# Two buffers for the folds' key and query weights in place of four, two more for the perceptron's weight sums, and earlier loads for both

## The chip, the cores and the metric

The kernel runs on one core of a Trainium2 chip. The metric is the device time of one execution in microseconds (us); the median of three runs of the kernel before is 1908.61 us (1908.29 to 1909.63). TensorE does the matmuls, VectorE (DVE), ScalarE (ACT) and GpSimd (POOL) work on tiles in SBUF, and SyncE (SP) issues nearly all DMAs. Each engine takes its instructions strictly in the order in which the program lists them, so an instruction that waits holds up everything behind it on the same engine; for SP that means that a DMA that may not start yet holds up every DMA listed after it.

## The reference

A pre-norm block on 2048 tokens of width 1024: linear attention with 32 heads, whose queries and keys go through a small matrix per head and two softmaxes (of p and of -p), then a perceptron of width 3584 with ReLU. Inputs and outputs are float32.

```python
qkv = x_normed @ wqkv                                  # heads of 32
pq, pk = q @ w_phi[h], k @ w_phi[h]
phi = concat(softmax(p), softmax(-p))                  # for pq and pk
kv, z = phi_k^T v, sum over tokens of phi_k
o = (phi_q kv) / (phi_q z + 1e-6)
h = x + o @ wo
out = h + relu(layernorm(h) @ w1) @ w2
```

## The kernel before, in words

TensorE multiplies in a 32-bit format with shortened mantissas (`F32R`), so each operand is split into a high and a low part and each product takes three matmuls (`mm3`, lines 181 to 184): high by high, high by low, low by high. The second one (line 183) is the first to read the low part of the weights.

**Steps and items.** All work is listed by hand in the order of "items". An item of the first phases is one output tile of 128 tokens by 512 columns and has 8 "steps"; a step is one `mm3`, that is three matmuls of 512 columns. `when(step, f, ...)` lists the call `f` behind the matmuls of the step with that number. Items 0 to 31 (steps 0 to 255) compute keys and values of the first eight token tiles, eight items for each of four column groups s; items 32 to 47 (steps 256 to 383) the queries, in two column groups; then keys and values, and queries, of the other eight tiles; then attention, output projection and the perceptron. So the weights change at steps 64, 128, 192, 256 and 320.

**Weights.** `Units` loads a 128x512 piece of weights into one of 6 `raw` buffers (lines 324 and 325 for keys and values, 328 for queries), ACT copies its high part into one of 10 `w` buffers (line 125), and POOL or DVE, in turn, subtracts to get the low part (line 129). Eight `w` are in use by the eight items of a column group, so two of the next group's pieces are made early, and each of the other six only after the last use of a piece of the present group: piece k is then listed for conversion 10 steps ahead of its use.

**Folds.** The small matrix per head is multiplied into wqkv once: `fold_all(p)` (32x32 matmuls, line 290), p = 0 to 7. Fold 0 is done at the start in another way (lines 279 and 382 to 406). For p = 1 to 7 they stand at the steps `FOLD_STEPS = 31, 64, 104, 144, 176, 206, 232`. Their operands are two `wt` tiles of 512 KB each, loaded by `wt_load(p)` on SP (line 274) into four buffers: two of `p` beside two of `p + 1`. `wt_load(p + 1)` stands 12 steps behind `fold_all(p)`; `wt_load(1)` is listed at the very start, ahead of the third token tile. The result goes through DVE (line 300) and is stored by SP 6 steps after the fold (line 311); it may be loaded as weights 17 steps after the fold.

**Sums of the perceptron's weights.** The perceptron uses a scheme with 7 products for 8 blocks, which needs differences of blocks of w1 and w2. They are made in the shadow of the first phases by 56 tasks, one for every 10 steps (n = 0 to 55, lines 1087 to 1094): `t_load` has SP load a tile `b` of 512 KB (line 351), 7 to 10 steps later POOL makes four subtractions in it (`t_sum`, line 361), and 13 steps after the load `t_store` writes it back to DRAM (line 364). There are two `b` buffers, so the load of task n waits until the store of task n - 2 has landed, and that store is listed 7 steps ahead of it. The tasks from n = 28 on stand 64 steps later.

**Other work in these steps.** POOL also adds up the keys' features (`zacc`, line 452, 18 steps behind the start of an item), and makes a power for the layer norm (lines 230 to 232). The `fold` pool, with `wphi`, `wt`, `bd` and `wp`, is closed at step 256, and its place is taken by tiles of the attention.

Of the kernel before, what the change touches and what calls it, by code (L numbers as in the profile page):

```python
# [9 lines left out]
F32 = mybir.dt.float32  # L10
F32R = mybir.dt.float32r
AF = mybir.ActivationFunctionType
ALU = mybir.AluOpType
AX = mybir.AxisListType

P = 128
S = 2048
D = 1024
# [122 lines left out]
def kernel(  # L141
# [12 lines left out]
    v, act, pool, pe, sp = nc.vector, nc.scalar, nc.gpsimd, nc.tensor, nc.sync  # L154
# [34 lines left out]
    def do(n, k, f, *args):  # L189
        at[n, k].append((f, args))  # L190
# [14 lines left out]
    td = {(w, p): dram.tile([P, 4, 512], F32, name=f"t{w}_{p}") for w in (1, 2) for p in range(NP)}  # L205
# [55 lines left out]
    tsp = kps.enter_context(tc.tile_pool(name="tsum", bufs=1, side="right"))  # L261
    folds = ExitStack()
    fp = folds.enter_context(tc.tile_pool(name="fold", bufs=2))
# [6 lines left out]
    def wt_load(p, eng):  # L270
        for i in range(2):
            j = 8 + 2 * p + i if p < 4 else 2 * (p - 4) + i
            t = fp.tile([P, D], F32, name="wt", bufs=4)
            eng.dma_start(t, wqkT[j])
            wt_of[p, i] = t

# [67 lines left out]

    tsum = {}

    def t_load(w, p, j):
        cols = slice(256 * j, 256 * (j + 1))
        b = tsp.tile([P, 4, 256], F32, name="b", bufs=2)
        src = (w1 if w == 1 else w2)[2 * p:2 * p + 2, :, :, cols]  # L350
        sp.dma_start(b, src.rearrange("a b p f -> p (a b) f"))
        for r in range(2):
            for c in range(2):
                tsum[j, r, c] = b[:, 2 * c + r if w == 1 else 2 * r + c, :]
        tsum[j] = b

    def t_sum(j, n):

        out, a, b = [((0, 0), (0, 1), (0, 0)), ((0, 1), (1, 1), (0, 1)),
                     ((1, 1), (1, 1), (0, 0)), ((1, 0), (1, 0), (1, 1))][n]  # L360
        pool.tensor_tensor(out=tsum[j, *out], in0=tsum[j, *a], in1=tsum[j, *b], op=ALU.subtract)  # L361

    def t_store(w, p, j):
        sp.dma_start(td[w, p][:, :, 256 * j:256 * (j + 1)], tsum[j])

    first_raw = {}

    def first_values():

        for k in range(0, NK, 2):  # L370
            if k == 4:
                ln_load(("x", 1), x_part(1))
            place = W.raws.take()
            t = place[1]
            sp.dma_start(t.rearrange("p (k f) -> p k f", k=2), wv[0, k:k + 2].rearrange("k p f -> p k f"))
            for i in range(2):
                first_raw[k + i] = t[:, 256 * i:256 * (i + 1)], place
        W.loaded = W.done = NK
# [474 lines left out]
    def item(gen, *args, keys):  # L853
        items.append((gen, args + (keys,)))
        steps.extend((k,) for k in keys)
        return len(items) - 1

    kv_n, q_n, wo_n, up_n, down_n = {}, {}, {}, {}, {}
# [9 lines left out]
    for b, tiles in enumerate(groups):  # L868
        for hf in range(2):

            pairs = b == 0 and hf == 0
            for j in range(0, 4, 2 if pairs else 1):
# [3 lines left out]
                for half in range(2):  # L876
                    n = item(wo_pair, tiles[j:j + 2], hf, half, keys=[("wo", hf, 4 * half + k // 2) for k in range(8)])
# [26 lines left out]
    def when(step, f, *args):  # L904

        if step < 8 * first_up:
            do(step // 8, step % 8, f, *args)
        else:
            do(first_up + (step - 8 * first_up) // 4, step % 4, f, *args)
# [4 lines left out]
    for t in range(1, NT):  # L914
        n = t - 1 if t < HT else q_n[1, t - HT] + 1
# [3 lines left out]
        else:  # L919

            early = 80 + 16 * (t - HT)
# [14 lines left out]
    for i, j in enumerate((2, 3, 0, 1)):  # L936
        do(1 + i // 2, 2 + 4 * (i % 2), first_copy, j)
        when(8 * (1 + i // 2) + 2 + 4 * (i % 2) + 3, fold_store, 0, 2 * j, 2)
    when(40, fold_ready, 0)
    for p, n in enumerate(FOLD_STEPS, 1):  # L940
        when(n, fold_all, p)
        when(n, fold_turn, p)
        when(n + 6, fold_store, p)
        when(n + 17, fold_ready, p)
        if p < 7:
            when(n + 12, wt_load, p + 1, sp)


    for (hf, s, t), n in kv_n.items():
# [111 lines left out]
    def up_step(b, p, m):  # L1061

        return up0 + 4 * (up_n[b, p, m] + 1 - first_up)

    for j, m in enumerate(UP):

        for g in range(2):
            step = up0 + (8 * j + (-62, -32)[g] if j < 4 else 6 * (j - 4) + 10 + 2 * g)
# [4 lines left out]
            step = up_step(0, NP - 1, m) + 3 * j  # L1073
# [13 lines left out]
    for n, (w, p, j) in enumerate((w, p, j) for w in (1, 2) for p in range(NP) for j in range(2)):  # L1087
        step = 24 + 10 * n
        if step > 8 * q_n[1, 0] - 20:
            step += 64  # L1090
        when(step, t_load, w, p, j)
        for k in range(4):
            when(step + 7 + k, t_sum, j, k)
        when(step + 13, t_store, w, p, j)

    for b in range(2):
        for m in DOWN:
            n = down_n[b, m, NP - 1] + 1
            name, more = {1: "x1", 5: "x4", 6: "x2", 4: "x3"}.get(m), \
# [18 lines left out]
    sp.dma_start(wphi, w_phi.rearrange("(j i) e f -> i e j f", i=4))  # L1118
    ln_load(("x", 0), [x[0:P, 0:512], x[0:P, 512:1024]])
    wt_load(0, sp)  # L1120
    first_values()
    wt_load(1, sp)
    ident = consts.tile([P, P], F32, name="ident")
    make_identity(nc, ident)
    ones = consts.tile([P, P], F32, name="ones")
# [7 lines left out]
    for i in range(4):  # L1133
        r = slice(32 * i, 32 * (i + 1))
# [76 lines left out]
```

## Time and profile before

| | |
|---|---|
| median of the runs | 1908.61 us |
| time of the profiled execution | 1908.77 us |
| its span, first to last instruction | 1907.0 us |
| mean granted TensorE clock | 0.998 |
| DVE, ACT, POOL busy | 1048.1, 740.3, 974.6 us |
| HBM read, written | 292.68 MB, 137.36 MB |
| `b` loads, `b` stores | 56 of 512 KB each, on SP |
| `wt` loads | 16 of 512 KB, on SP |

The profile lists each engine's busy time, groups of instructions by line, waits with what ended them, and a timeline. A row of the timeline has the start in us, the duration in us, the engine, the line, the operation, output and inputs, and in square brackets how long the engine had been idle just before and which work ended that. "SPq" is the issuing of a DMA by SyncE, not the transfer. A row of a waits view has the time waited in all, how often, and the longest. In the windows view the bracketed counts are instructions; the last three columns are the granted TensorE clock, the share of the 16 DMA engines that was busy, and their rate.

### The profile page before, as it was taken

To read this page: it belongs to the slowest core of one execution; us is meant where nothing else is said; L and a number is where in the kernel's file an instruction comes from. 1 tells how busy PE (TensorE), PEld (TensorE's weight loads), DVE (VectorE), ACT (ScalarE), POOL (GpSimd) and SP (SyncE) were. 2 spreads that over 40 slices of the span, in tenths; PEclk is the share of its full clock that TensorE was granted. 3 is DMA by queue.
4 is the path that set the end of the run, shared out by engine and by line. 5 is a ranking of instruction groups with operands and counts; after the bars stand their busy time and mean duration, and the time that the engine had idled before them with its cause. 6 is when DMAs were issued, how large, how long until landed. Compare 5 with 4: busy or idle time off the path is not lost.

```text
span 1907.0 us, 31851 instructions
## 1 busy us (share of the span) xinstructions
PE 1882.6 (99%) x11640; PEld 1539.3 (81%) x11640; DVE 1048.1 (55%) x1685; ACT 740.3 (39%) x1258; POOL 974.6 (51%) x961
## 2 busy tenths in 40 slices
PE   8999999999999999999999999999999999999999
PEld 7767778877778887888888888888888888888887
DVE  6777678767679866545644564344433433343333
ACT  5322226222223222255445564444444444444442
POOL 4677752789955988423333222222244444444443
PEclk9999999999999999999999999999999999999999
DMA  6888786666565667696776897566677677877775
GB/s 213 267 259 304 229 274 198 211 193 209 196 209 186 214 210 241 213 304 219 258 252 227 279 289 223 174 195 192 217 238 227 192 238 231 244 213 220 216 215 178
DMA packets 292365, 432.17 MB, mean 227 GB/s; under 512 B 24048, under 2 KB 150000, under 8 KB 292208
## 3 DMA queue, kind: packets, MB, share of 16 engines
q1 hardware_dynamic: 275312, 413.36, 68.8%
q10 hardware_dynamic: 16896, 16.78, 2.5%
q8 instruction: 91, 1.49, 0.3%
q14 instruction: 66, 0.54, 0.1%
HBM read 292.68 MB, written 137.36 MB: 226 GB/s over the span
## 4 chain that ended last, share of the span: by engine, by line
PE 79%; POOL 12%; DMA 6%; issue 2%; DVE 1%; SPq 1%; ACT 0%; POOLq 0%; ACTq 0%; DVEq 0%
PE mm L182 19%; PE mm L183 19%; PE mm L184 19%; PE ac L183 4%; PE ac L182 4%; PE ac L184 4%; POOL b L361 3%; PE tp L183 2%; PE tp L184 2%; PE tp L182 2%; DMA b<-in_w_dram 2%; POOL w L129 2%; POOL ez L574 2%; DMA t<-b 1%; PE tp L245 1%
## 5 line engine op out<-in xcount | busy, mean ns | idle before, releaser
L129 POOL TENSOR_TENSOR w<-raw,w 128x512 fp32r<-128x512 f32 x355 | 474.7, 1339 | 716.1 <-ACT w L125 671.9
L125 ACT ACTIVATE w<-raw 128x512 fp32r<-128x512 f32 x686 | 408.9, 626 | 514.3 <-PE mm L184 248.1
L129 DVE TENSOR_TENSOR w<-raw,w 128x512 fp32r<-128x512 f32 x331 | 272.3, 823 | 529.2 <-ACT w L125 526.0
L183 PE MATMUL mm<-w,xT 128*128 128x512 f32 x768 | 302.2, 393 | 9.0 <-POOL w L129 8.7
L182 PE MATMUL mm<-w,xT 128*128 128x512 f32 x768 | 309.0, 402 | 0.0
L184 PE MATMUL mm<-w,xT 128*128 128x512 f32 x768 | 300.7, 392 | 0.0
L182 PE MATMUL mm<-hT,w 128*128 128x512 f32 x672 | 262.6, 391 | 0.0
L183 PE MATMUL mm<-hT,w 128*128 128x512 f32 x672 | 261.6, 389 | 0.5 <-DVE hT L753 0.5
L184 PE MATMUL mm<-hT,w 128*128 128x512 f32 x672 | 261.6, 389 | 0.0
L361 POOL TENSOR_TENSOR b<-b 128x256 f32<-128x256 f32 x224 | 179.9, 803 | 100.2 <-DMA b<-in_w_dram 90.3
L183 PEld LDWEIGHTS mm<-w,xT 128*128 128x128 f32 x768 | 144.9, 189 | 43.1 <-POOL w L129 13.5
L182 PEld LDWEIGHTS mm<-w,xT 128*128 128x128 f32 x768 | 144.9, 189 | 34.9 <-issue 4.2
L184 PEld LDWEIGHTS mm<-w,xT 128*128 128x128 f32 x768 | 144.8, 189 | 30.8
L182 PE MATMUL mm<-w 128*128 128x512 f32 x392 | 152.5, 389 | 0.0
L183 PE MATMUL mm<-w 128*128 128x512 f32 x392 | 152.5, 389 | 0.0
L184 PE MATMUL mm<-w 128*128 128x512 f32 x392 | 152.5, 389 | 0.0
L183 PEld LDWEIGHTS mm<-hT,w 128*128 128x128 f32 x672 | 126.2, 188 | 26.6 <-DVE hT L753 0.9
L184 PEld LDWEIGHTS mm<-hT,w 128*128 128x128 f32 x672 | 126.1, 188 | 26.5
L182 PEld LDWEIGHTS mm<-hT,w 128*128 128x128 f32 x672 | 126.2, 188 | 25.8
L182 PEld LDWEIGHTS mm<-w 128*128 128x128 f32 x392 | 73.6, 188 | 15.3
L184 PEld LDWEIGHTS mm<-w 128*128 128x128 f32 x392 | 73.6, 188 | 15.3
L183 PEld LDWEIGHTS mm<-w 128*128 128x128 f32 x392 | 73.6, 188 | 15.3
(169 smaller groups left out, 3102.4 us busy)
## 6 DMA issues: line engine op xcount, KB each, us to landing
raw<-t SPq DMA_DIRECT2D x224, 256.0 KB, 3.8
raw<-ad SPq DMA_DIRECT2D x196, 256.0 KB, 3.0
raw<-in_w_dram SPq DMA_DIRECT2D x168, 256.0 KB, 3.1
b<-in_w_dram SPq DMA_DIRECT2D x56, 512.0 KB, 4.2
t<-b SPq DMA_DIRECT2D x56, 512.0 KB, 4.7
ad<-c SPq DMA_DIRECT2D x112, 256.0 KB, 3.5
ad<-s SPq DMA_DIRECT2D x84, 256.0 KB, 3.8
ed<-qe ACTq DMA_DIRECT2D x32, 512.0 KB, 4.7
```

The costliest lines, as they stand in the source:

```text
L125: nc.scalar.activation(w[:, 0, :], raw[1], AF.Copy)
L129: eng.tensor_tensor(out=w[:, 1, :], in0=raw[1], in1=w[:, 0, :].bitcast(F32), op=ALU.subtract)
L182: pe.matmul(ps, a_hi, b_hi, start=first, stop=False, skip_group_check=more)
L183: pe.matmul(ps, a_hi, b_lo, start=False, stop=False, skip_group_check=more)
L184: pe.matmul(ps, a_lo, b_hi, start=False, stop=last, skip_group_check=more)
L245: pe.transpose(pt[:, k, :], xn[:, (4 * j + k) * P:(4 * j + k + 1) * P], ident)
L361: pool.tensor_tensor(out=tsum[j, *out], in0=tsum[j, *a], in1=tsum[j, *b], op=ALU.subtract)
L574: pool.tensor_tensor(out=ez, in0=e_q[u].rearrange("p (i h) s f -> p i (h s f)", i=4)[:, 2 * j:2 * j + 2, :], in1=zb[:, q, None, 256 * r:25 ...
```

## The change

Four edits, all in the order and the buffers of DMAs:

- `wt` has two buffers in place of four, so the loads for fold p + 1 overwrite the tiles that fold p reads.
- `wt_load(p + 1)` stands 3 steps behind `fold_all(p)` in place of 12, and `wt_load(1)` at step 2 in place of the start.
- The memory of the two `wt` buffers goes to two more `b` buffers in the `fold` pool. Of the tasks whose step lies below 8 * 32 - 16 = 240 (n = 0 to 21), those with n % 4 of 2 or 3 use them, the others the two old ones; so the load of task n waits there for the store of task n - 4.
- For the same tasks the load stands 8 steps sooner, at step 16 + 10n, with sums and store where they were. The tasks from n = 22 on keep their two buffers and their places.

The rest of the diff carries the task's number through the names.

```diff
-            t = fp.tile([P, D], F32, name="wt", bufs=4)
+            t = fp.tile([P, D], F32, name="wt", bufs=2)
...
-    def t_load(w, p, j):
+    def t_load(w, p, j, early):
         cols = slice(256 * j, 256 * (j + 1))
-        b = tsp.tile([P, 4, 256], F32, name="b", bufs=2)
+        b = (fp if early else tsp).tile([P, 4, 256], F32, name="b", bufs=2)
...
-                tsum[j, r, c] = b[:, 2 * c + r if w == 1 else 2 * r + c, :]
-        tsum[j] = b
+                tsum[w, p, j, r, c] = b[:, 2 * c + r if w == 1 else 2 * r + c, :]
+        tsum[w, p, j] = b
...
+    when(2, wt_load, 1, sp)
     for p, n in enumerate(FOLD_STEPS, 1):
...
         if p < 7:
-            when(n + 12, wt_load, p + 1, sp)
+            when(n + 3, wt_load, p + 1, sp)
...
-        when(step, t_load, w, p, j)
+        free = step < 8 * q_n[0, 0] - 16
+        when(step - 8 if free else step, t_load, w, p, j, free and n % 4 > 1)
         for k in range(4):
-            when(step + 7 + k, t_sum, j, k)
+            when(step + 7 + k, t_sum, (w, p, j), k)
         when(step + 13, t_store, w, p, j)
...
     wt_load(0, sp)
     first_values()
-    wt_load(1, sp)
```

More of the change, by code (lines that the diff above doesn't have):

```diff
@@ L353, in t_load, with t_sum @@
             for c in range(2):
-                tsum[j, r, c] = b[:, 2 * c + r if w == 1 else 2 * r + c, :]
-        tsum[j] = b
-    def t_sum(j, n):
+                tsum[w, p, j, r, c] = b[:, 2 * c + r if w == 1 else 2 * r + c, :]
+        tsum[w, p, j] = b
+    def t_sum(u, n):
         out, a, b = [((0, 0), (0, 1), (0, 0)), ((0, 1), (1, 1), (0, 1)),
                      ((1, 1), (1, 1), (0, 0)), ((1, 0), (1, 0), (1, 1))][n]
-        pool.tensor_tensor(out=tsum[j, *out], in0=tsum[j, *a], in1=tsum[j, *b], op=ALU.subtract)
+        pool.tensor_tensor(out=tsum[*u, *out], in0=tsum[*u, *a], in1=tsum[*u, *b], op=ALU.subtract)
     def t_store(w, p, j):
-        sp.dma_start(td[w, p][:, :, 256 * j:256 * (j + 1)], tsum[j])
+        sp.dma_start(td[w, p][:, :, 256 * j:256 * (j + 1)], tsum[w, p, j])
     first_raw = {}
```

## The prediction

> **What bounds the kernel now.** I read the page first, then the waits of TensorE, then the windows by stage, and at last the timelines around each gap.
>
> ```profile
> span 1907.0 us, 31851 instructions
> PE 1882.6 (99%) x11640; PEld 1539.3 (81%) x11640; DVE 1048.1 (55%) x1685; ACT 740.3 (39%) x1258; POOL 974.6 (51%) x961
> ...
> 122.32 0.50 PE L183 MATMUL mm<-w,xT 128*128 128x512 f32 x1 [1.21 <-POOL w L129]
> 126.61 0.50 PE L183 MATMUL mm<-w,xT 128*128 128x512 f32 x1 [2.63 <-POOL w L129]
> 129.34 0.80 PE L183 MATMUL mm<-w,xT 128*128 128x512 f32 x1 [0.34 <-POOL w L129]
> 179.50 0.50 PE L183 MATMUL mm<-w,xT 128*128 128x512 f32 x1 [0.78 <-POOL w L129]
> 208.91 0.45 PE L290 MATMUL tp<-wt,wphi 32*32 32x256 f32 x8 [0.89 <-DMA wt<-in_wqkT_dram]
> 211.61 0.45 PE L290 MATMUL tp<-wt,wphi 32*32 32x256 f32 x8 [1.86 <-DMA wt<-in_wqkT_dram]
> 236.61 0.50 PE L183 MATMUL mm<-w,xT 128*128 128x512 f32 x1 [0.73 <-POOL w L129]
> ```
>
> TensorE is the bound: outside its busy time only 1907.0 - 1882.6 = 24.4 us are left. So this change, which touches no matmul, can win only what TensorE loses to waiting, plus what its clock loses. Seven of the gaps lie in the stretch that the change touches (steps 16 to 240, up to about 220 us): 1.21 + 2.63 + 0.34 = 4.18 at the change of weights at step 128, 0.78 at step 192, 0.89 + 1.86 = 2.75 at fold 7, 0.73 at step 256.
>
> ```profile
> core 0: us, PE busy (x) PEld busy (x) DVE busy (x) ACT busy (x) POOL busy (x), PEclk, DMA share, GB/s
> 120.00:127.30 7.30, 3.46 (x14) 2.21 (x13) 5.26 (x12) 1.26 (x2) 7.15 (x8) 1.00 0.80 292
> 127.30:130.70 3.40, 3.06 (x8) 1.94 (x7) 0.00 (x0) 0.00 (x0) 3.19 (x3) 0.50 0.83 231
> 205.00:212.60 7.60, 4.85 (x123) 2.84 (x121) 1.95 (x6) 1.02 (x2) 4.15 (x5) 1.00 1.00 368
> 212.60:216.00 3.40, 3.40 (x10) 2.62 (x9) 3.26 (x7) 0.00 (x0) 2.86 (x4) 0.50 0.18 52
> ```
>
> The windows show a second loss: twice, right behind the larger gaps, the granted clock is 0.50 for 3.40 us. Half of TensorE's busy time there is lost: 3.06 / 2 + 3.40 / 2 = 3.2 us.
>
> **Why the operand is late.** At step 128 TensorE waits for POOL's low parts, so POOL's own timeline is next, with SP's behind it.
>
> ```profile
> 97.97 3.50 POOL L361 TENSOR_TENSOR b<-b 128x256 f32<-128x256 f32 x4 [7.29 <-DMA b<-in_w_dram]
> ...
> 114.06 2.71 POOL L361 TENSOR_TENSOR b<-b 128x256 f32<-128x256 f32 x3 [4.04 <-DMA b<-in_w_dram]
> 116.73 1.29 POOL L452 TENSOR_TENSOR zacc<-zacc,kphi 128x512 f32<-128x512 f32 x1
> ...
> 121.00 1.27 POOL L129 TENSOR_TENSOR w<-raw,w 128x512 fp32r<-128x512 f32 x1
> ...
> 124.85 1.71 POOL L129 TENSOR_TENSOR w<-raw,w 128x512 fp32r<-128x512 f32 x1
> ...
> 128.01 1.27 POOL L129 TENSOR_TENSOR w<-raw,w 128x512 fp32r<-128x512 f32 x1
> ...
> 169.89 0.74 POOL L361 TENSOR_TENSOR b<-b 128x256 f32<-128x256 f32 x1 [2.89 <-DMA b<-in_w_dram]
> ```
>
> ```profile
> 113.78 1.99 ACT L125 ACTIVATE w<-raw 128x512 fp32r<-128x512 f32 x3 [0.35 <-PE mm L184]
> ```
>
> ```profile
> 93.22 0.53 SPq L364 DMA_DIRECT2D t<-b  x1
> 99.22 0.39 SPq L351 DMA_DIRECT2D b<-in_w_dram  x1
> ```
>
> ```profile
> POOL b L361 <- DMA b<-in_w_dram: 34.1, 11, 7.3
> ...
> SPq L351 <- DMA t<-b: 56.9, 16, 5.9
> SPq L274 <- PE mm L184: 1.5, 3, 0.7
> ```
>
> The last fence is the waits of 40 to 240 us. POOL stands 34.1 us before sums whose tile has not landed; SP stands 56.9 us before tile loads whose buffer is still being stored. The two buffers close a ring: store at 93.22, and the load that needs its buffer only at 99.22. Ahead of step 128 POOL loses 7.29 + 4.04 = 11.33 us so. ACT has the high part of the first of three POOL pieces at 113.78 + 1.99 / 3 = 114.4, but POOL comes to it at 121.00, and has no gap between 114.06 and then: it is behind by 6.6 us, and each piece goes straight into a gap of TensorE.
>
> **The sums, with the new loads.** Steps become times by TensorE's rows:
>
> ```profile
> 112.17 0.39 PE L182 MATMUL mm<-w,xT 128*128 128x512 f32 x1
> ...
> 116.93 0.39 PE L182 MATMUL mm<-w,xT 128*128 128x512 f32 x1
> ...
> 120.72 0.40 PE L182 MATMUL mm<-w,xT 128*128 128x512 f32 x1
> ```
>
> 21 matmuls, or 7 steps, take 4.76 us: 0.68 us a step. The matmul at 120.72 opens step 130. A load that stands 15 steps ahead of its sums instead of 7 has 10.2 us instead of 4.8, and its buffer's store is listed 19 steps (12.9 us) ahead of it instead of 7 (4.8).
>
> ```profile
> DMA to landing us min/median/max: 3.2/4.4/7.9
> ```
>
> That row is for loads and stores of `b`: at worst 7.9, below 10.2 and below 12.9, so both waits go for the tasks up to n = 21, as long as SP is on time. POOL does the same work in the same order and can only come earlier. It would reach the first piece 121.0 - 11.3 = 109.7, before ACT has it; so it starts at 114.4. From there, by the listed order and 1.28 us a piece, 0.74 a sum, 1.29 a `zacc`: first piece done at 115.7 (needed at 120.95, the second matmul of step 130), a sum, `zacc`, a sum and the second piece by 119.8 (needed two steps later, 122.3), two sums and the third by 122.5 (needed 123.7). The last has 1.2 us to spare, no more; one slow row (1.71 in place of 1.28) eats a third of it. I count the 4.18 us as won and hold 0.6 back as a small new gap. At step 192 the 0.78 goes too: POOL's 2.89 us wait at 167 to 169.89 lies ahead of it. Worst case, the pieces come no earlier: nothing won here; best case, all 4.96.
>
> **The folds' tiles.**
>
> ```profile
> 199.01 0.38 SPq L311 DMA_DIRECT2D wpq<-wp  x1
> 199.49 0.53 SPq L351 DMA_DIRECT2D b<-in_w_dram  x1
> 202.61 0.53 SPq L364 DMA_DIRECT2D t<-b  x1
> 203.19 1.90 SPq L274 DMA_DIRECT2D wt<-in_wqkT_dram  x2
> ```
>
> ```profile
> DMA to landing us min/median/max: 5.0/6.9/8.3
> ```
>
> The second fence is the landing of `wt` loads. Fold 7 wants its tiles at 208.91 - 0.89 = 208.0, and two loads whose issue takes from 203.19 to 205.09, 4.8 us ahead of that at best, cannot be there. The new place, step 209, lies 9 steps (6.1 us) sooner, ahead of the store of fold 6 (1 MB, step 212, here 199.01) and of a `b` load and a `b` store. With SP as late as now the loads are issued 10.9 to 9.0 us ahead of the need, above the 8.3 of the slowest landing; with SP on time, at step 209 for a fold at step 232, it is 23 steps, 15.6 us. Both hold however much earlier TensorE then comes, since they count from its step: the 2.75 us go. The lower bound is that the crowd at 205 to 212.6 (DMA share 1.00) eats it: nothing won.
>
> **What the two `wt` buffers cost.** The load now overwrites what the fold three steps ahead reads, so SP, where it is more than three steps ahead of TensorE, stands until TensorE comes. SP did that for 1.5 us in all so far. Behind it stand tile loads (2.3 us of slack: 10.2 - 7.9), token tiles and the fold's store, which waits for that fold anyway. How far is SP ahead?
>
> ```profile
> 41.30 0.45 PE L290 MATMUL ac<-wt,wphi 32*32 32x256 f32 x8
> ```
>
> ```profile
> 41.92 0.71 SPq L351 DMA_DIRECT2D b<-in_w_dram  x1
> ```
>
> Fold 1 (step 31) begins at 41.30 and SP issues the load of step 34 at 41.92: three steps, 2.0 us, less the 0.6 it is behind. So it would stand some 1 us at fold 1. Upper bound: SP can pass POOL by at most the 10 steps between two stores, which puts the stand at 10 - 3 = 7 steps, 4.8 us, six times. What could reach TensorE through it is a raw piece of the next weights:
>
> ```profile
> 104.75 0.58 SPq L324 DMA_DIRECT2D raw<-wpk  x1
> ```
>
> ```profile
> DMA to landing us min/median/max: 1.9/3.4/8.1
> ```
>
> The last raw piece for step 128 is issued at 104.75, 9.0 us before ACT begins on them at 113.78, and lands in 3.4 (second fence, all `raw` tiles): 5.6 us to spare, more than the 4.8. So I take 0. `wt_load(1)` at step 2 waits for fold 0, which stands ahead of step 0, and fold 1 comes at step 31: 29 steps, 19.7 us, for a landing of 8.3; 0.
>
> **The sum.** 4.18 + 0.78 + 2.75 of gaps, 3.2 of clock, 0.11 us (0.34 - 0.23, the first spacing behind a gap) for each of six gaps = 0.7: 11.6 us, less 0.6 held back and 0.2 for the rest of the clock: -10.8 us. The 0.73 at step 256 and all later gaps stay, since the tasks from n = 22 on keep their ring. The profiled execution took 1908.77 us for a span of 1907.0 and stands 0.16 above the median, so I subtract from the median: 1908.6 - 10.8 = **1897.8 us**.
>
> About the clock: here gaps of 2.63 and 1.86 us were each followed by 3.40 us at 0.50, while the gap of 0.78 was not. [...]
>
> **Rivals.**
> (a) One of the two places stays: the tiles of fold 7 land late again because the DMA engines are full there (share 1.00). For: the rate of 368 GB/s in 205 to 212.6. Against: the move of 6.1 us. Time: 1897.8 + 2.75 + 1.7 + 0.2 = 1902.5.
> (b) The half-clock stretches stay without the gaps: 1897.8 + 3.2 = 1901.0. Against: they follow the two largest gaps of this stretch and no others.
> (c) No gain: SP issues the loads no sooner, since each store in its queue waits for POOL, and POOL is full (7.15 of 7.30 us at 120 to 127.3), so its pieces are as late as now; and fold 7 stays by (a). Only the 0.78 goes: 1907.8. Against: the 11.33 us that POOL idles before step 128.
> (d) Slower: SP's stand at the moved `wt` loads grows until the raw pieces of the next column group come late. It decides where SP stands beyond the 5.6 us, a lead of 3 + 8 = 11 steps; then each change of weights at steps 64, 128, 192 and 256 costs what step 128 costs now, 4.18 + 1.5 of clock = 5.7: 22.8 in place of the 7.2 that steps 128, 192 and 256 cost today, less 4.4 for fold 7: +11.2, 1919.8. For: six such loads, each at the head of one queue. Against: the lead of three steps at fold 1, and the bound of 10 steps.
>
> **How the numbers follow.** Forecast 0.64, with its own range 1894.9 (nothing held back, and 2 us more in the later gaps) to 1900.5; (a) 0.10, (b) 0.05, (c) 0.11, (d) 0.10. About 0.2% (3.8 us) is what a measurement of this kernel can tell from no change. Faster by more: forecast, (a) and (b), 0.79; within: (c), 0.11; slower: (d), 0.10. The range takes in forecast, (a) and (b) and goes to 1905.5 for a mixture with (c).
>
> **What would show it.** In the changed profile: no wait of SP's load (line 351) for a store, and none of POOL's sums for a tile, before about 220 us; POOL's three pieces at step 128 from about 114.5; no gap of 0.3 us or more of TensorE between 60 and 215 us; clock 1.00 throughout; fold 7's tiles issued before 200 us. SP's wait for TensorE at the `wt` loads rises from 1.5 us to some 10. It is wrong if a gap behind POOL at 120 to 130 stays over 1 us, or a new one follows a fold.

## The result and the profile after

The changed kernel takes 1897.48 us (median of four, 1895.23 to 1898.54) against 1908.45 us (four, 1905.38 to 1909.63): a ratio of 0.9943, 95% interval 0.9926 to 0.9961. Run twice more beside other kernels it gave 0.9942 (0.9927 to 0.9957) and 0.9942 (0.993 to 0.9955). The forecast was 1897.8 us.

From the changed kernel's page, its span and busy times:

```profile
span 1896.2 us, 31858 instructions
PE 1880.8 (99%) x11640; PEld 1539.3 (81%) x11640; DVE 1050.0 (55%) x1685; ACT 740.3 (39%) x1258; POOL 975.8 (51%) x961
```

All TensorE gaps between 60 and 260 us and three later ones, from the timeline:

```profile
124.42 0.50 PE L183 MATMUL mm<-w,xT 128*128 128x512 f32 x1 [0.51 <-POOL w L129]
225.56 0.50 PE L183 MATMUL mm<-w,xT 128*128 128x512 f32 x1 [0.72 <-POOL w L129]
...
516.49 0.50 PE L183 MATMUL mm<-w,xT 128*128 128x512 f32 x1 [1.38 <-POOL w L129]
621.91 0.34 PE L632 MATMUL tp<-qe,kvL 32*32 32x128 f32 x8 [0.45 <-POOL ez L574]
840.37 0.50 PE L183 MATMUL mm<-hT,w 128*128 128x512 f32 x1 [0.26 <-DVE hT L753]
```

The three gaps at step 128 (4.18 us) are one of 0.51; those at step 192 and at fold 7 are gone; that at step 256 stands, 0.72 us long. The matmul behind that one is also a mark to compare by: it stood at 236.61 and stands at 225.56, so 11.05 us are won by then. The gaps at fold 7 and at step 128 had a half clock behind them; the same stretches now, in the windows view:

```profile
core 0: us, PE busy (x) PEld busy (x) DVE busy (x) ACT busy (x) POOL busy (x), PEclk, DMA share, GB/s
120.00:127.30 7.30, 6.79 (x31) 5.26 (x30) 5.74 (x14) 1.54 (x3) 7.14 (x7) 1.00 0.44 127
127.30:130.70 3.40, 3.40 (x27) 2.58 (x28) 1.98 (x6) 1.15 (x2) 3.05 (x7) 1.00 0.99 321
205.00:212.60 7.60, 7.60 (x35) 6.29 (x34) 4.78 (x11) 1.02 (x2) 3.46 (x4) 1.00 0.99 310
212.60:216.00 3.40, 3.40 (x17) 2.82 (x16) 2.02 (x5) 2.18 (x4) 0.55 (x1) 1.00 0.51 181
...
513.70:517.10 3.40, 1.90 (x8) 1.01 (x7) 0.92 (x1) 0.00 (x0) 3.40 (x5) 1.00 0.43 140
517.10:520.50 3.40, 3.40 (x10) 2.63 (x9) 1.02 (x1) 0.00 (x0) 3.40 (x3) 0.50 0.80 278
```

The clock is full where it was halved. It is halved at another place in this execution, at 517 us, behind the gap of 1.38 us there, which costs half of 3.40, 1.7 us. The waits between 40 and 215 us say why POOL is on time:

```profile
POOL b L361 <- DMA b<-in_w_dram: 0.9, 1, 0.9
...
SPq L364 <- POOL b L361: 38.7, 14, 6.8
...
SPq L274 <- PE mm L290: 6.7, 7, 3.2
SPq L274 <- PE tp L290: 3.2, 1, 3.2
...
SPq L351 <- DMA t<-b: 2.6, 2, 2.2
```

POOL's 34.1 us before tiles (up to 215 us they were the same 34.1) are 0.9; SP's 56.0 us (up to 215 us) before tile loads whose buffer is still being stored are 2.6; and SP now stands 9.9 us before TensorE's folds, since `wt` has only two buffers. SP waits elsewhere instead: its tile stores wait 38.7 us for POOL's sums, 16.8 before the change. POOL's timeline around step 128 shows the piece that was late:

```profile
114.57 1.30 POOL L129 TENSOR_TENSOR w<-raw,w 128x512 fp32r<-128x512 f32 x1 [1.85 <-ACT w L125]
115.83 1.19 POOL L361 TENSOR_TENSOR b<-b 128x256 f32<-128x256 f32 x1
116.98 1.78 POOL L452 TENSOR_TENSOR zacc<-zacc,kphi 128x512 f32<-128x512 f32 x1
118.72 1.19 POOL L361 TENSOR_TENSOR b<-b 128x256 f32<-128x256 f32 x1
119.87 1.74 POOL L129 TENSOR_TENSOR w<-raw,w 128x512 fp32r<-128x512 f32 x1
121.57 1.56 POOL L361 TENSOR_TENSOR b<-b 128x256 f32<-128x256 f32 x2
123.09 1.28 POOL L129 TENSOR_TENSOR w<-raw,w 128x512 fp32r<-128x512 f32 x1
```

Before, POOL came to the first piece at 121.00, out of a backlog. Now it waits 1.85 us for ACT and starts at 114.57; the third piece ends at 124.37, 0.5 us late.

### The profile page after: what moved, and what is told of

Its sections match the earlier page's. It is cut to its first block, busy times and chain, and to the rows that moved or that the text cites. A ratio compares the mean times of both kernels' runs of the same rounds, so it can differ in the third digit from the quotient of the medians.

```text
span 1896.2 us, 31858 instructions
## 1 busy us (share of the span) xinstructions
PE 1880.8 (99%) x11640; PEld 1539.3 (81%) x11640; DVE 1050.0 (55%) x1685; ACT 740.3 (39%) x1258; POOL 975.8 (51%) x961
## 4 chain that ended last, share of the span: by engine, by line
PE 84%; POOL 6%; DMA 4%; issue 3%; DVE 2%; ACT 0%; SPq 0%; POOLq 0%; DVEq 0%; ACTq 0%
PE mm L182 21%; PE mm L183 21%; PE mm L184 21%; PE ac L184 4%; PE ac L182 4%; PE ac L183 4%; PE tp L182 2%; PE tp L184 2%; PE tp L183 2%; POOL w L129 2%; POOL b L361 2%; DMA b<-in_w_dram 1%; PE tp L245 1%; POOL ez L574 1%; DMA t<-b 1%
## 5 line engine op out<-in xcount | busy, mean ns | idle before, releaser
L183 PEld LDWEIGHTS mm<-w,xT 128*128 128x128 f32 x768 | 144.7, 188 | 36.8 <-POOL w L129 7.3
L452 POOL TENSOR_TENSOR zacc<-zacc,kphi 128x512 f32<-128x512 f32 x60 | 81.9, 1364 | 9.4 <-DVE kphi L444 9.4
L182 PEld LDWEIGHTS mm<-w 128*128 128x128 f32 x392 | 73.6, 188 | 15.3
L184 PEld LDWEIGHTS mm<-w 128*128 128x128 f32 x392 | 73.6, 188 | 15.3
```

What stands on the lines that cost most here:

```text
L182: pe.matmul(ps, a_hi, b_hi, start=first, stop=False, skip_group_check=more)
L183: pe.matmul(ps, a_hi, b_lo, start=False, stop=False, skip_group_check=more)
L184: pe.matmul(ps, a_lo, b_hi, start=False, stop=last, skip_group_check=more)
L452: pool.tensor_tensor(out=zacc[s], in0=zacc[s], in1=phi_of[key], op=ALU.add)
```

## The experiments

There were eleven runs, of eight variants (one of them twice) and of the changed kernel itself (twice), in three groups; the kernels of a group ran on one chip beside the kernel before, and each ratio is to that kernel there (median 1905.6, 1906.04 and 1907.15 us).

**The folds' part alone.** The tile loads of the sums keep two buffers and their old places:

```diff
-        free = step < 8 * q_n[0, 0] - 16
+        free = False
```

> The folds' part alone: two wt buffers and their earlier loads, while the tile loads of the sums keep two buffers and their old places. Theory (each gap belongs to its own part): fold 7 no longer waits for its tiles (2.75 us) and the half clock behind it goes (1.7 us), but POOL keeps its waits for b (about 34 us between 40 and 240 us), the three gaps at step 128 (about 4.2 us) stay with their half clock, and the 0.8 at step 192: 1908.5 - 4.5 = 1904 us. Rival (fold 7's tiles are late only because SP stands before stores of b): the fold's gap stays too, 1908 us. Rival (the two wt buffers make SP stand in a harmful way, hidden in the full change by the other part): above 1910 us.

Measured: 1909.0 us, ratio 1.0016 (1.0004 to 1.0029): a little slower than before, where 4.5 us were expected to be won. The part that was expected of fold 7 is there: it waits no longer, and the clock from 200 to 216 us is 1.00. But POOL is later at the changes of weights at steps 128 and 192, from the timelines of TensorE and of POOL:

```profile
121.19 0.50 PE L183 MATMUL mm<-w,xT 128*128 128x512 f32 x1 [0.21 <-POOL w L129]
128.27 0.79 PE L183 MATMUL mm<-w,xT 128*128 128x512 f32 x1 [5.42 <-POOL w L129]
181.29 0.50 PE L183 MATMUL mm<-w,xT 128*128 128x512 f32 x1 [2.31 <-POOL w L129]
184.21 0.51 PE L183 MATMUL mm<-w,xT 128*128 128x512 f32 x1 [1.25 <-POOL w L129]
```

```profile
119.85 1.29 POOL L129 TENSOR_TENSOR w<-raw,w 128x512 fp32r<-128x512 f32 x1
123.92 0.73 POOL L361 TENSOR_TENSOR b<-b 128x256 f32<-128x256 f32 x1 [2.78 <-DMA b<-in_w_dram]
```

The gaps there are 9.19 us in place of 4.96. In the profiled execution this takes back what fold 7 won: the matmul at step 256 stands at 236.84, 0.2 us later than before the change. The reason lies in SP's queue:

```profile
109.46 0.93 SPq L274 DMA_DIRECT2D wt<-in_wqkT_dram  x2
110.48 0.52 SPq L364 DMA_DIRECT2D t<-b  x1
...
118.37 0.38 SPq L351 DMA_DIRECT2D b<-in_w_dram  x1
```

The same load before the change:

```profile
115.34 0.37 SPq L351 DMA_DIRECT2D b<-in_w_dram  x1
```

The moved `wt` loads, 1 MB, now go out right ahead of a tile's store, the next tile's load waits for that store until 118.37, and POOL then waits 2.78 us for the tile between the first piece and the second. SP's stand before the folds, the second rival, is not the reason: between 40 and 240 us SP waits 0.9 us for folds there. So the two parts are not independent: with two `b` buffers, loads that were put ahead of a tile's store were paid by POOL.

**The sums' part alone.** Four `b` buffers and earlier tile loads; the folds' loads at their old distance, with two buffers:

```diff
-            when(n + 3, wt_load, p + 1, sp)
+            when(n + 12, wt_load, p + 1, sp)
```

> The sums' part alone: four b buffers and loads 8 steps sooner, while the folds' loads go back to 12 steps behind the fold (with two buffers, which are free by then). Theory (SP on time): the gaps at steps 128 and 192 go but for some 0.5 us; the loads for fold 7 are issued around step 218, 14 steps or 9.5 us ahead of it, for a landing of 5.0 to 8.3, so its gap goes as well: 1897 to 1899 us, so that the place of the folds' loads adds nothing to it. Rival (the DMA engines are full there and the 9 steps are needed): fold 7 keeps its 2.75 us and the half clock, 1902 us.

Measured: 1895.92 us, ratio 0.995 (0.9933 to 0.9968), with gaps below 240 us of 0.50 and 0.72 only. Fold 7 does not wait. Run again beside the whole change:

> The sums' part alone again, now beside the whole change. Theory (the moved loads of the folds add nothing once SP is on time): the same time as the whole change, within 1.5 us. Rival (they cost something, by SP's stand before TensorE, 9.9 us in the changed profile against 2.6 here): faster than the whole change by 2 us or more. Rival (they bring something): slower by 2 us or more.

Measured: 1896.81 us (0.9949, 0.9934 to 0.9963) beside 1895.53 us of the whole change (0.9942, 0.9927 to 0.9957); the whole change beside it had this on record:

> The changed kernel itself, beside the three others on one chip. Every theory: 0.994 to 0.996 of the kernel before, one gap of about 0.5 us at step 128 and one of about 0.7 at step 256 below 240 us.

So the sums' part is the whole gain. The folds' earlier loads add nothing that can be told from noise: the medians of the two lie 1.3 us apart, and the whole change's executions (1894.85 to 1896.21 us) lie within the range of the other's (1894.83 to 1898.72). The folds' part gives the two buffers whose memory the `b` tiles take; no run tried four `wt` beside four `b`.

**Four buffers without the earlier loads.**

```diff
-        when(step - 8 if free else step, t_load, w, p, j, free and n % 4 > 1)
+        when(step, t_load, w, p, j, free and n % 4 > 1)
```

> Four b buffers, but the tile loads at their old places, 7 steps (4.8 us) ahead of the sums. Theory (it is the ring of two buffers that makes SP late): SP's waits before stores are nearly gone, POOL's waits for tiles fall from 34 us to some 15 (landing 4.4 to 7.9 against 4.8), POOL's first piece at step 128 comes at most 2 us after ACT's high part, gaps there below 1.5 us: 1898 to 1900 us. Rival (the 8 steps matter as much as the buffers): POOL stays late by 4 us or more at step 128 and the gaps with the half clock stay, 1903 us or more.

Measured: 1902.4 us, ratio 0.998 (0.9969 to 0.9992), a third of the gain. I had bet on 1898 to 1900 us and on gaps below 1.5 us at step 128; the rival said 1903 us or more with POOL 4 us late. It came out between the two, nearer to the rival: POOL comes to the first piece at 117.69, some 3.2 us after ACT's high part. TensorE's gap at step 128, with a half clock behind it (the matmul there takes 0.79 us; behind the gap of 0.51 in the changed kernel it takes 0.50), and POOL's timeline:

```profile
125.83 0.79 PE L183 MATMUL mm<-w,xT 128*128 128x512 f32 x1 [3.32 <-POOL w L129]
```

```profile
111.26 2.70 POOL L361 TENSOR_TENSOR b<-b 128x256 f32<-128x256 f32 x3 [2.82 <-DMA b<-in_w_dram]
...
117.69 1.28 POOL L129 TENSOR_TENSOR w<-raw,w 128x512 fp32r<-128x512 f32 x1
121.45 0.74 POOL L361 TENSOR_TENSOR b<-b 128x256 f32<-128x256 f32 x1 [2.47 <-DMA b<-in_w_dram]
```

Another gap of 1.17 us stays at step 192; fold 7 does not wait. SP's wait of loads for stores is gone (1.0 us), but POOL still waits 36.8 us for tiles between 40 and 240 us, where it was 34.1. Now they are late for another reason: the load is listed 7 steps, 4.8 us, ahead of its use, and the tile loads between 40 and 215 us take a median of 6.9 us to land, where it was 4.4 before the change:

```profile
b<-in_w_dram SPq DMA_DIRECT2D x21, 512.0 KB, 6.9
t<-b SPq DMA_DIRECT2D x20, 512.0 KB, 5.6
```

**Two buffers with earlier loads.**

```diff
-        when(step - 8 if free else step, t_load, w, p, j, free and n % 4 > 1)
+        when(step - 6 if free else step, t_load, w, p, j, False)
```

> Two b buffers with the loads 6 steps sooner (more would make a load wait for a store listed behind it). Theory (the ring is the limit): each load is issued when the store ahead of it has landed, as before, so POOL waits about as before, SP's waits for stores rise above 57 us between 40 and 240 us, and the gaps at step 128 stay: 1902 to 1906 us. Rival (only the place in the queue matters): as the full change, 1897 to 1899 us.

Measured: 1927.62 us, ratio 1.0116 (1.0096 to 1.0137): far slower, which neither theory said. The waits of SP and POOL between 40 and 240 us, and the worst gap, at step 192:

```profile
SPq L351 <- DMA t<-b: 118.1, 20, 9.0
```

```profile
POOL b L361 <- DMA b<-in_w_dram: 55.2, 15, 7.7
```

```profile
191.07 0.79 PE L183 MATMUL mm<-w,xT 128*128 128x512 f32 x1 [7.80 <-POOL w L129]
```

A load that stands one step behind the store of its own buffer here holds SP for most of that store's landing, 5.9 us on the average (118.1 / 20; the stores' median landing is 7.0), and everything behind it: a store goes out at 103.64, the load behind it at 110.86, the next piece of weights at 111.34. So POOL does not wait about as before, as the theory had it, but 55.2 us in place of 34.1. Here earlier places without more buffers are worse than nothing, and more buffers without earlier places are worth a third.

**POOL's lateness put back by hand.** Six idle additions (nothing reads their result) of 128x512 on POOL, in the changed kernel, at step 119 or at step 84; the edit for step 119:

```diff
+    junk = fp.tile([P, 512], F32, name="junk", bufs=1)
+    pool.memset(junk, 0.0)
+    for _ in range(6):
+        when(119, lambda: pool.tensor_tensor(out=junk, in0=junk, in1=junk, op=ALU.add))
```

> The changed kernel with six idle subtractions' worth of POOL work (128x512, about 1.29 us each, 7.7 us in all) put in at step 119, ahead of the three pieces of weights for step 128. Theory (TensorE loses what POOL is late by at these pieces, and the clock halves behind it): the first piece begins near 120.5 us in place of 114.6, gaps of 5 to 7 us at step 128 with 3.4 to 6.8 us at half clock behind them: 6 to 10 us over the changed kernel. Rival (the gaps came from full DMA queues and not from POOL's lateness): POOL makes it up, under 2 us.

> The same six instructions at step 84, after which POOL has 9.9 us of waits up to step 120. Theory (only lateness that is still there at a change of weights counts): no new gap, time within 1 us of the changed kernel. Rival (any work added to POOL here costs, since POOL is the second bound): 4 to 8 us more.

Measured: at step 119, 1902.22 us (0.9978, 0.9968 to 0.9987), 6.7 us above the changed kernel's 1895.53 in the same group; at step 84, 1895.86 us (0.9943, 0.9929 to 0.9958), no difference. With the work at step 119, in POOL's and TensorE's timelines:

```profile
112.54 7.28 POOL L1082 TENSOR_TENSOR junk<-junk 128x512 f32<-128x512 f32 x6
119.78 1.73 POOL L129 TENSOR_TENSOR w<-raw,w 128x512 fp32r<-128x512 f32 x1
```

```profile
121.57 0.50 PE L183 MATMUL mm<-w,xT 128*128 128x512 f32 x1 [0.54 <-POOL w L129]
125.86 0.80 PE L183 MATMUL mm<-w,xT 128*128 128x512 f32 x1 [2.64 <-POOL w L129]
```

The first piece comes 5.6 us later than in the changed kernel of this group (114.18), near the 121.00 of the kernel before, and the gaps are back: 0.54 + 2.64 = 3.2 us, in place of 0.51, with a half clock behind them (0.60 from 126.0 to 129.4 us). The gaps are smaller than the 5 to 7 that I had put down, since the second and third piece caught up some of it. 2.7 us of gap and 1.7 of clock make 4.4 of the 6.7, and by the matmul at step 256 the profiled execution is 4.9 us behind the changed kernel's in this group (230.03 against 225.13); in this execution the clock was also halved at 521 us, behind a gap of 1.40 us that the changed kernel's execution in this group had without a half clock, another 1.7.

**SP's stand.** The folds' loads one step behind the fold in place of three:

```diff
-            when(n + 3, wt_load, p + 1, sp)
+            when(n + 1, wt_load, p + 1, sp)
```

> The folds' loads one step behind the fold in place of three, so that SP stands two steps longer before TensorE. Theory (the stand costs nothing, since nothing behind it is due): SP's waits for TensorE at line 274 rise from 10 us to between 14 and 19, no new gap, time within 1 us of the changed kernel. Rival (SP's stand eats the slack of the loads behind it): POOL waits for tiles again, gaps at step 128, 2 us or more slower.

Measured: 1895.92 us (0.9943, 0.993 to 0.9955) beside the changed kernel's 1896.27 (0.9942, 0.993 to 0.9955), for which this stood on record:

> The changed kernel again, as the measure for the two beside it: 0.994 to 0.996 of the kernel before.

SP stands 15.4 us (10.3 + 5.1) in place of 9.6, and no gap follows. A stand of this length costs nothing here.

**A try at what is left.** The low parts of query pieces 2, 5 and 7 on DVE, in both halves (so far 2 and 5 in the first):

```diff
-                key[:2] == ("q", 0) and key[-1] in (2, 5)
+                key[0] == "q" and key[-1] in (2, 5, 7)
```

> The changed kernel with the low parts of query pieces 2, 5 and 7 on DVE in both halves (so far 2 and 5 in the first half and none in the second). Theory (what is left of the gaps at steps 256 and 640, 0.7 and 1.4 us with a half clock in some executions, is POOL's load at a change of weights): both gaps go, 2 to 4 us faster than the changed kernel. Rival (DVE is as late there as POOL): the gaps stay or move to DVE, same time or slower.

Measured: 1896.11 us (0.9941, 0.9927 to 0.9954), the same as the changed kernel. The two gaps did go (0.73 and 1.40 us; 0.16 is left of the second), and came back in the attention:

```profile
600.15 0.47 PE L632 MATMUL tp<-qe,kvL 32*32 32x128 f32 x8 [2.23 <-POOL ez L574]
```

```profile
600.10:606.80 6.70, 6.65 (x107) 5.16 (x108) 6.67 (x14) 3.93 (x8) 3.19 (x4) 0.50 0.05 8
```

TensorE reaches the attention 3.6 us sooner (597.41 against 601.01 in the changed kernel of this group) and waits 2.23 us there (0.39 in that kernel), with 6.7 us of half clock behind it. Why POOL's work there does not come sooner with it was not tried. No version that ran is measurably faster than the changed kernel.

## Why the prediction was right

- *What bounds the kernel.* Right: TensorE's gaps and the half clock behind them were all there was to win. The two runs with idle work on POOL show the mechanism alone: some 7 us of POOL's time cost nothing at step 84 and 6.7 us at step 119.
- *Step 128.* 4.18 us with 0.6 held back: 0.51 is left. The first piece starts at 114.57 (forecast 114.4). The chain behind it was too short in the forecast, since two of the four sums that I put at 0.74 took 1.19, the `zacc` 1.78 and the second piece 1.74: the third piece ends at 124.37 and not at 122.5. It was needed at 124.42 - 0.51 = 123.9. The sign "no gap of 0.3 us or more" was missed by it, though the sum had held 0.6 back.
- *Step 192 and fold 7.* 0.78 and 2.75 us went as forecast, so rival (a) falls; the tiles of fold 7 are issued at 185.83, 15.6 us ahead of the fold at 201.38, as worked out for SP on time. But for fold 7 the forecast credits the move of its loads, and the sums' part alone does it too: SP on time is enough. What I called enough by itself, the move of 9 steps, does end that gap by itself, and the loss at steps 128 and 192 takes it all back (1.0016).
- *Clock.* Both half-clock stretches went with the gaps, so rival (b) falls. The other executions agree: the mean granted clock was 1.000 in all ten of the changed kernel in the two later groups and 0.996 to 1.000 in the 49 of the kernel before. The 3.2 us of clock are thus a figure of one execution; in the group of 1906.04 us the one execution before at 1.000 took 1903.88 us, still 8.4 above the changed kernel's median there. That the clock would be 1.00 throughout was wrong for the profiled execution: one stretch of 3.4 us came behind the gap of 1.38 us at 516 us. By step 256 the changed kernel is 11.05 us ahead, for a forecast of 10.8. Three later gaps of the kernel before, and the second of them in the changed kernel:

```profile
631.33 0.34 PE L632 MATMUL tp<-qe,kvL 32*32 32x128 f32 x8 [0.49 <-POOL ez L574]
728.44 0.66 PE L245 MATMUL tp<-ident,xin 128*128 128x128 f32 x4 [1.67 <-DVE oT L650]
851.15 0.50 PE L183 MATMUL mm<-hT,w 128*128 128x512 f32 x1 [0.47 <-DVE hT L753]
```

```profile
717.86 0.66 PE L245 MATMUL tp<-ident,xin 128*128 128x128 f32 x4 [0.49 <-DVE oT L650]
```

The matmul at 631.33 stands at 621.91 now, only 9.4 us sooner: the new half clock took 1.7. Of the gap of 1.67 us at 728.44 only 0.49 is left, which I had not counted, and that gives most of it back: 851.15 became 840.37, 10.8 us. In two other executions of the changed kernel this gap is 1.45 and 0.84 us, so that it shrank is not shown to be the change's doing. That the total lies closer to the forecast than its terms do is luck.
- *The landing.* I took 7.9 us, the slowest landing of before, as the bound under the 10.2 us of lead. With more buffers the landing itself grew: the median of the tile loads between 40 and 215 us was 4.4, 4.9 and 3.7 us in the three kernels with two buffers, and 6.9 and 6.8 in the two with four that differ in the loads' places. That it is the larger number of loads in flight is my reading; no run shows it by itself. In the changed kernel:

```profile
b<-in_w_dram SPq DMA_DIRECT2D x21, 512.0 KB, 6.8
...
DMA to landing us min/median/max: 3.4/6.3/10.8
```

 The slowest landing of `b` loads and stores together is 10.8, above the lead if it was a load; it cost only one wait of 0.9 us, but the argument had no such margin. A landing of 6.9 us against a lead of 4.8 also fits with how little four buffers at the old places won.
- *SP's stand.* Forecast some 10 us and no cost: 9.9 us, and none even at 15.4. The longest single stand is 3.2 us, below the bound of 4.8. Rival (d) falls. Rival (c) was right that stores wait for POOL (38.7 us), but with four buffers and earlier places the next tiles are there all the same, and POOL's waits for them went from 34.1 to 0.9 us. The slower outcome that lay near was another one, which I had not named: tile loads that stand right behind the store of their own buffer (1.0116).
- *Independent terms.* The sum added the parts as if each had its own price. The total came out, the parts did not: -9.7 and +3.4 us alone by their medians, -10.5 and -10.9 together in the two later groups.

## What to carry to other kernels

A ring of buffers on an in-order DMA queue has two lengths: how far the load is listed behind the store that frees its buffer, and how far ahead of its use. Compare both with the landing measured under load: here a load 4.8 us ahead of its use, with a median landing of 6.9, kept a third of the gain, and one a step behind its store made the kernel 1.2% slower. Here lengthening one by shortening the other, or moving other loads ahead of the store, cost more than it brought (1.0116 and 1.0016). To see whether an engine's lateness matters, put idle work on it at two places, one right ahead of the consumer and one with slack behind it.

## What the runs showed of the hardware

The clock was 0.50 for 3.40 us behind gaps shorter than that, but not behind each: in the kernel before it was halved behind 1.86 and 2.63 us, in the run of the folds' part not behind 2.31 us (the matmul behind the next gap there, at 184.21, took 0.51 us; in a half clock of the kernel before, at 129.34, such a one took 0.80), and the gap at some 515 us had a half clock in the changed kernel's first profile (1.38 us long) and none in its other two (1.40 us). So two executions of one program can differ by 1.7 us (half of 3.40) from this alone, and the length of a gap alone does not decide it: 1.38 us were once enough, 2.31 us once were not. What decides between such gaps stays open.

The half clock also lasted twice as long once: 6.7 us in the last experiment, behind a gap of 2.23 us, where it was 3.40 behind one of 2.63. In the kernel before, the mean granted clock of the third group's nine executions lay between 0.997 and 0.999 with times from 1903.81 to 1909.68, while all five of the changed kernel's there had 1.000 (1896.07 to 1897.09): part of what the change took away is the scatter.
